# Attention results evacuated by ScalarE and normalised in place on GpSimd, thresholds on GpSimd, and both instruction orders written out as tables

## The chip, the cores and the metric

One core of a Trainium2 chip runs the whole program. The metric is device time in microseconds; lower is better. The five instruction queues that appear below are TensorE (PE), VectorE (DVE), ScalarE (ACT), GpSimd (POOL) and the DMA-issuing SyncE (SP).

## What is computed

```python
def _attn_ref(q, k, v, tau):            # q, k, v: 4 x 8 x 576 x 64
    scale = 1.0 / np.sqrt(q.shape[-1])
    scores = scale * np.matmul(q, k.transpose(0, 1, 3, 2))
    thresh = np.max(scores, axis=-1, keepdims=True) - tau
    scores = np.where(scores >= thresh, scores, -1000000000.0)
    scores = scores - np.max(scores, axis=-1, keepdims=True)
    attn = np.exp(scores)
    attn = attn / (np.sum(attn, axis=-1, keepdims=True) + 1e-09)
    return np.matmul(attn, v)
```

The result, as 2304 tokens of 512 numbers, goes through `g = max(h, 0) + alpha * min(h, 0)` with `h = x @ w_in`, then `g @ w_out`, and once more through such a pair of products (512 to 2048 to 512) with SiLU between them. All inputs are 32-bit floats.

## The kernel before

The program has two stages, one after the other. The first is attention, the second the four large matrix products ("the products stage").

**Attention.** Two heads of one batch entry make a pair; there are 16 pairs `i`, and each has nine tiles `t` of 64 query rows for both heads, so 144 units `u`. For one unit PE writes the scores into PSUM (`qkmm`, tile `s`; the tiles 0 to 7 go two at a time, tile 8 alone with twice the contraction), DVE scales them into SBUF and takes their extreme value (`maxi`, tile `x`), ACT takes the exponential (`expo`, tile `e`, or `z` for the ninth tile), and DVE compares `x` with the threshold and multiplies `e` by the result, with the row sum as a by-product (`mask`). The threshold itself is a sum of one or two columns, `thr`, on ACT. When a pair's nine masks are done, DVE takes reciprocals of the row sums in two pieces (`recip`), ACT copies them out into the tiles `rb` (`spread`, two pieces), PE transposes masked exponentials and reciprocals (`trans`), ACT copies the transposed blocks from PSUM (`copy`, tiles `pt` and `px`), PE multiplies by the values (`pv` in five steps, `pv8` for the ninth tile), and DVE multiplies the product in PSUM by the transposed reciprocals into the activations `X` (`evac`, and two 64x64 products `evac8`).

In the same stretch the weights of the first products are converted (`conv`: seven tiles, partly on POOL) and three sets of activations are split in a high and a low part (`piece`).

**The products stage** runs the 2304 tokens in three parts. Each product is made of three matrix multiplications of 384 columns over high and low parts; most 2x2 block products use seven block products in place of eight, with sums of blocks formed on DVE or POOL.

**What sets the order.** For attention PE's order is the string `ORDER` (`Q2:5` the scores of tiles 2 and 3 of pair 5, `T` a transposition, `P` a `pv` step); a list scheduler in the program, `plan`, places the other engines' work by due times, which the string `SHIFT1` corrects. For the products stage `plan_late` does the same with `SHIFT` and picks for each two-operand step marked BOTH whether DVE or POOL runs it (`SIDE` fixes some of them). Each engine then runs its instructions in that order, and semaphores hold what isn't ready.

Of the kernel before, what the change touches and what calls it, by code (L numbers as in the profile page):

```python
# [49 lines left out]
NRAW = 2  # L50
ST = ((False, True, True, True), (True,) * 4)
# [1322 lines left out]
```

## Time and profile before

| | us |
|---|---|
| median of 3 runs | 990.46 (988.98 to 991.07) |
| the profiled execution's own time | 991.97 |
| its span in the profile | 990.0 |
| busy: PE, DVE | 967.0, 857.6 |
| busy: ACT, POOL | 651.6, 295.8 |

The span starts with the first instruction of the program and ends with the last; the profiled execution lasts 2 us more. It stands 1.5 us above the median, so a difference that is worked out on the trace is taken off both alike. Attention takes the first 279 us, the products stage the rest. Busy time counts an instruction from its start to its end; neighbours on one engine overlap a little (two scalings of `x` start 0.74 us apart and last 0.82 us each), so a row's mean is somewhat more than what the next instruction waits for.

### The profile page before, as it was taken

The numbers are of one execution on the slowest core, as the hardware profiler recorded it, in microseconds if no ns is written. First come the engines' busy times: TensorE is split into PE (matmuls) and PEld (weight loads), VectorE is DVE, ScalarE is ACT, GpSimd is POOL, SyncE is SP. The second block draws the span as 40 slices with busy tenths as digits, with TensorE's granted clock in tenths as the row PEclk, the third lists the DMA queues.
The fourth block names the chain that finished last, engine by engine and source line by source line (L and its number), as shares of the span: only waits on it lengthen the run. The fifth ranks groups of instructions, "written<-read, shape, count | busy, mean of one in ns | idle before, by whom it ended". The sixth has DMA issues, their size and how long they took to land.

```text
span 990.0 us, 18130 instructions
## 1 busy us (share of the span) xinstructions
PE 967.0 (98%) x6781; PEld 857.7 (87%) x6781; DVE 857.6 (87%) x1740; ACT 651.6 (66%) x1179; POOL 295.8 (30%) x227
## 2 busy tenths in 40 slices
PE   8999899999999999999999999999999999999998
PEld 4555555555679999999999999999999999999998
DVE  6999999999879867988899999999788997788655
ACT  6997888989877666455555556777675555555442
POOL 0003111031033222344543344322333124544432
PEclk9999999999999999999999999999999999999999
DMA  3132322331365876677777887547766776655743
GB/s 117 47 113 75 127 68 93 109 91 47 117 250 228 287 265 215 237 249 263 260 240 237 260 267 273 180 183 274 277 238 220 262 261 254 230 213 196 249 160 112
DMA packets 46055, 194.11 MB, mean 196 GB/s; under 512 B 5392, under 2 KB 8592, under 8 KB 45968
## 3 DMA queue, kind: packets, MB, share of 16 engines
q1 hardware_dynamic: 43936, 187.97, 54.0%
q0 software_dynamic: 1728, 4.72, 2.5%
q8 instruction: 53, 0.87, 0.4%
q10 hardware_dynamic: 304, 0.28, 0.1%
q14 instruction: 34, 0.28, 0.1%
HBM read 150.48 MB, written 37.75 MB: 190 GB/s over the span
## 4 chain that ended last, share of the span: by engine, by line
PE 74%; DVE 14%; issue 5%; ACT 4%; DMA 3%; SPq 0%; DVEq 0%; ACTq 0%
PE ab L593 27%; PE c L593 17%; PE y L593 16%; PE y L1082 5%; DVE e L748 5%; DVE x L722 5%; PE s L708 4%; PE pv L815 3%; PE t L790 2%; DMA xs<-xd 2%; ACT e L735 1%; ACT pt L440 1%; DMA r<-r 1%; PE t L822 0%; DVE X L834 0%
## 5 line engine op out<-in xcount | busy, mean ns | idle before, releaser
L593 PE MATMUL ab<-xs,w 128*128 128x384 f32 x1728 | 316.0, 335 | 1.9 <-ACT su L440 1.3
L593 PEld LDWEIGHTS ab<-xs,w 128*128 128x128 f32 x1728 | 300.8, 188 | 3.7 <-ACT su L440 1.9
L593 PE MATMUL y<-g,w 128*128 128x384 f32 x840 | 158.8, 335 | 1.2 <-DVE X L1099 1.2
L440 ACT ACTIVATE g<-r 128x768 fp32r<-128x768 f32 (+1 forms) x143 | 112.9, 796 | 57.3 <-POOL r L1126 11.6
L593 PEld LDWEIGHTS y<-g,w 128*128 128x128 f32 x840 | 146.8, 188 | 1.5 <-DVE X L1099 1.5
L542 POOL TENSOR_TENSOR cw<-cw 128x128 f32<-128x128 f32 (+1 forms) x77 | 44.8, 581 | 253.6 <-DVE cw L528 158.5
L708 PE MATMUL s<-raw 64*128 64x288 f32 (+1 forms) x576 | 114.0, 432 | 5.0 <-DVE x L722 4.1
L722 DVE TENSOR_SCALAR_CACHE_REDUCE x<-s,nsc 128x576 f32<-128x576 f32 x144 | 112.9, 812 | 5.7 <-PE s L708 4.5
L593 PE MATMUL c<-g,w 128*128 128x384 f32 x612 | 115.7, 334 | 0.0
L748 DVE SCALAR_TENSOR_TENSOR e<-x,m,e 128x577 f32<-128x577 f32 x128 | 112.2, 907 | 2.9 <-ACT m L742 2.3
L440 ACT ACTIVATE su<-ab 128x384 f32<-128x384 f32 x144 | 69.4, 488 | 61.9 <-PE ab L593 55.7
L593 PEld LDWEIGHTS c<-g,w 128*128 128x128 f32 x612 | 107.0, 188 | 0.0
L735 ACT ACTIVATE e<-x,m 128x576 f32<-128x576 f32 x128 | 96.9, 777 | 15.2 <-DVE x L722 14.7
L1099 DVE TENSOR_TENSOR X<-y,X 128x384 f32<-128x384 f32 x150 | 81.7, 553 | 23.0 <-PE y L593 22.1
L1134 POOL TENSOR_TENSOR g<-r,g 128x768 fp32r<-128x768 f32 x41 | 75.9, 1863 | 82.7 <-ACT g L440 27.6
L708 PEld LDWEIGHTS s<-raw 64*128 64x128 f32 (+1 forms) x576 | 66.3, 191 | 36.1 <-DVE x L722 24.9
L545 POOL TENSOR_TENSOR w<-cw,w 128x896 fp32r<-128x896 f32 (+1 forms) x28 | 58.8, 2099 | 126.1 <-ACT w L440 110.2
L790 PEld LDWEIGHTS t<-ident,e 64*128 64x128 f32 x1152 | 51.3, 139 | 38.9 <-ACT pt L440 13.8
L1134 DVE TENSOR_TENSOR g<-r,g 128x768 fp32r<-128x768 f32 x80 | 78.2, 981 | 5.4 <-ACT g L440 5.3
L593 PE MATMUL c<-xs,w 128*128 128x384 f32 x432 | 81.9, 336 | 0.5 <-DMA xs<-xd 0.5
L593 PEld LDWEIGHTS c<-xs,w 128*128 128x128 f32 x432 | 75.4, 188 | 1.7 <-issue 0.8
L440 ACT ACTIVATE pt<-t 128x512 f32<-128x512 f32 x128 | 70.6, 591 | 7.8 <-PE t L790 7.8
(100 smaller groups left out, 1459.3 us busy)
## 6 DMA issues: line engine op xcount, KB each, us to landing
xs<-xd SPq DMA_DIRECT2D x126, 768.0 KB, 5.7
xd<-xs SPq DMA_DIRECT2D x42, 768.0 KB, 4.3
raw<-in_w1i SPq DMA_DIRECT2D x16, 512.0 KB, 5.2
raw<-in_w1o SPq DMA_DIRECT2D x16, 512.0 KB, 4.2
raw<-in_w2i SPq DMA_DIRECT2D x16, 512.0 KB, 4.9
raw<-in_w2o SPq DMA_DIRECT2D x16, 512.0 KB, 4.4
rv<-in_v SPq DMA_DIRECT2D x16, 480.0 KB, 4.2
raw<-in_q SPq DMA_DIRECT2D x15, 320.0 KB, 3.4
```

Of the source, the lines that this page charges most:

```text
L440: e.activation(out=dst, in_=src, func=AF.Copy)
L542: st.append((both_step if both else port_step)(256 if len(o.shape) == 3 else 128, ["cv", "ce", "ch"], ["ce"], lambda e=V, o=o, a=a, b=b, o ...
L545: st.append(both_step(512 if plain else 896, k + [(key, 0)], [(key, 0)], lambda e: e.tensor_tensor(out=z[:, 1], in0=x, in1=z[:, 0].bitcast ...
L593: T.matmul(bank, WT_[ws[c]][:, x, AI[a], :], xs[:, y, c, :], start=start and k == 0, stop=stop and k == 5, skip_group_check=True,)
L708: T.matmul(SP[u + k][:, hf, :S // 2], RAW[i][p, 0, q], RAW[i][p, 1, c], start=True, stop=True)
L722: V.tensor_scalar(out=x.rearrange("p (a b) -> p a b", a=2), in0=SP[u][:, :, :S // 2], scalar1=nsc, scalar2=None, op0=ALU.mult, op1=ALU.min ...
L735: A.activation(out=ES[u], in_=xts[u % XB][:, 1:S + 1], func=AF.Exp, bias=mcol(u, 0), scale=-1.0)
L748: V.scalar_tensor_tensor(out=e, in0=x, scalar=mcol(u, 1), in1=e, op0=ALU.is_le, op1=ALU.mult, accum_out=mcol(u, 2))
L790: T.transpose(TP[n][h][:, c * 64:c * 64 + 64], x[p], ident[p, p])
L1082: T.matmul(yt, wview(ws[f])[:, a, i * 128:(i + 1) * 128], half(gs[f, k])[:, c], start=n == 0, stop=n == 3 * G - 1)
L1099: V.tensor_tensor(out=dst, in0=src, in1=dst, op=ALU.add))))
L1134: add(*both_step(2 * HN, kr + kg, kg, lambda e: e.tensor_tensor(out=x[:, 1], in0=RP[n], in1=x[:, 0].bitcast(F32), op=ALU.subtract)))
```

## The change

- `evac` becomes a plain ACT copy from PSUM to `X`; the product with the reciprocals is made afterwards on POOL, in place in `X`, in pieces of up to 256 columns (`shares`, `norm`: 40 pieces over the 16 pairs). `evac8` becomes one ACT copy; its normalisation moves ahead of the transposition, where POOL multiplies the ninth tile's exponentials by its reciprocals (`norm8`, 16 times).
- `thr` moves from ACT to POOL (80 times). `recip` and `spread` are one instruction each per pair in place of two; the reciprocals' transposition is five blocks wide in place of six.
- POOL's other two-operand work in attention is cut in four: 28 parts of the seven weight tiles, 20 parts of the three activation splits (the sums of weight blocks stay whole).
- A two-operand POOL instruction in attention now waits for the last DVE instruction with two SBUF operands that the order puts ahead of it (`held`), as the products stage did already. 55 such waits are added, in front of 100 instructions.
- Before attention a few instructions run once on constant data (on `pr`), behind PE's nine idle matmuls; two exponentials on constant data at the start of ACT's queue go.
- `ORDER` is another string, and `plan` and `plan_late` no longer search: `replay` reads the order of all engines from `TABLE1` and `TABLE2`, and the side of each BOTH step from `SIDE`. In the products stage the instructions and their number are the same; 194 of the 528 BOTH steps stand on POOL against 183 before, PE's steps move by three places on average.

```diff
-SHIFT1 = (
+TABLE1 = (
+    "070308020t0x0u0-JpJq0y0+0zJr0B0v13141011Js160w0C1715At18JtJuJvAu191B1E12JwJx1A1FAw1G011C1J1DAx1NJyJz"
...
+    flat = [(*ops[n][:3], [rank[d] for d in ops[n][3] if d in rank]) for n in names]
+    ring = {rank["t", k]: [rank[x] for x in f] for k, f in enumerate(free)}
+    out, at = replay(flat, numbers(TABLE1), None, dict.fromkeys(("PE", "DVE", "ACT", "POOL", "SP"), 0.0), 0.0, names, ring)
...
-            A.activation(out=stat(i)[:, 1, a:z], in_=stat(i)[:, 0, a:z], func=AF.Identity, bias=ptau, scale=1.0)
+            P.tensor_scalar(out=stat(i)[:, 1, a:z], in0=stat(i)[:, 0, a:z], scalar1=ptau, scalar2=None, op0=ALU.add)
...
+        def recip(i):
+            V.reciprocal(stat(i)[:, 2], stat(i)[:, 2])
+
+        def spread(i):
+            RS[i] = rbp.tile([128, 8, 64], F32, tag="rb", name="rb")
+            A.activation(out=RS[i], in_=stat(i)[:, 2, 1:9].unsqueeze(2).to_broadcast([128, 8, 64]), func=AF.Copy)
+
+        def norm8(i):
+            e = EP[i, 4][:, 1:S + 1]
+            P.tensor_scalar(out=e, in0=e, scalar1=stat(i)[:, 2, 0:1], scalar2=None, op0=ALU.mult)
...
+        def evac(i):
+            for p, o, c, n in parts(i):
+                A.activation(out=X[p][:, pairs[i][1], o:o + n], in_=AV[i][:, c:c + n], func=AF.Copy)
...
+        def norm(i, p, o, c, n):
+            x = X[p][:, pairs[i][1], o:o + n]
+            return P.tensor_tensor(out=x, in0=x, in1=PT[i, "r"][:, :4].rearrange("p a b -> p (a b)")[:, c:c + n], op=ALU.mult)
...
+            A.activation(out=X[x][:, hp, c0:c0 + 64], in_=TP[bank[i, "r"]][1][:, 384:448], func=AF.Copy)
...
+        n = (512 if plain else 896) // parts
+        for c in (slice(i * n, (i + 1) * n) for i in range(parts)):
+            st.append(both_step(n, k + [(key, 0)], [(key, 0)], lambda e, c=c: e.tensor_tensor(
+                out=z[:, 1, c], in0=x[:, c], in1=z[:, 0, c].bitcast(F32), op=ALU.subtract)))
...
+        pq = [psS.tile([128, 2, 512], F32, tag="s", name="s") for _ in range(2)]
+        for hf in range(2):
+            for c in range(2):
+                for r in range(2):
+                    p = slice(r * 64, r * 64 + 64)
+                    T.matmul(pq[r][c * 64:c * 64 + 64, hf, :S // 2], pr[p, :64], pr[p, :S // 2], start=True, stop=True)
...
+        held = seen = None
+        for e, c, fn in todo:
+            x = fn()
+            if c == "DVE+":
+                held = x
+            elif c == "POOL+" and held is not seen:
+                tc.add_manual_dep(x.ins, held.ins.name, mybir.DependencyInfo(
+                    mybir.DependencyClass.Sync, mybir.DependencyReason.DATA), reason="port")
+                seen = held
```

The following rows are the instructions themselves in their order; line numbers are those of the kernel they belong to. On DVE, before, around the end of the third pair (L722 is `maxi`, L748 `mask`, L754 `recip`, L834 `evac`, L842 `evac8`):

```order
L722 TENSOR_SCALAR x_169,m<-s,nsc 128x576
L722 TENSOR_SCALAR x_172,m<-s,nsc 128x576
L842 TENSOR_TENSOR X_73<-t,px 64x64 x2
L748 SCALAR_TENSOR_TENSOR e,m<-x_169,m,e 128x577
L722 TENSOR_SCALAR x_175,m<-s,nsc 128x576
L748 SCALAR_TENSOR_TENSOR e,m<-x_172,m,e 128x577
L754 RECIPROCAL m<-m 128x8
L722 TENSOR_SCALAR x_169,m<-s,nsc 128x576
L722 TENSOR_SCALAR x_178,m<-s,nsc 128x576
L834 TENSOR_TENSOR X_73<-pv,px 128x512
L748 SCALAR_TENSOR_TENSOR z,m<-x_175,m,z 128x577
```

And on DVE with the change, at the same pair (L597 is `maxi`, L623 `mask`, L628 `recip`):

```order
L623 SCALAR_TENSOR_TENSOR e,m<-x_172,m,e 128x577
L623 SCALAR_TENSOR_TENSOR z,m<-x_175,m,z 128x577
L597 TENSOR_SCALAR x_175,m<-s,nsc 128x576
L628 RECIPROCAL m<-m 128x9
L597 TENSOR_SCALAR x_172,m<-s,nsc 128x576
L623 SCALAR_TENSOR_TENSOR e,m<-x_169,m,e 128x577
L623 SCALAR_TENSOR_TENSOR e,m<-x_178,m,e 128x577
L597 TENSOR_SCALAR x_169,m<-s,nsc 128x576
L597 TENSOR_SCALAR x_178,m<-s,nsc 128x576
```

`evac` and `evac8` have left DVE's queue, and what stands in it is scalings and masks, mostly two and two.

On POOL, before, the first two weight tiles (L542 are the sums of weight blocks, L545 the low part of a converted tile):

```order
L545 TENSOR_TENSOR w_76<-cw,w_76 128x896
L542 TENSOR_TENSOR cw<-cw 128x128
L542 TENSOR_TENSOR cw<-cw 128x256
L542 TENSOR_TENSOR cw<-cw 128x128
L545 TENSOR_TENSOR w_77<-cw,w_77 128x896
```

And on POOL with the change, at the second weight tile (L617 is `thr`, L636 `norm8`, L720 `norm`, L412 and L417 the former L542 and L545):

```order
L636 TENSOR_SCALAR z<-z,m 128x576
L412 TENSOR_TENSOR cw<-cw 128x128
L617 TENSOR_SCALAR m<-m,ptau 128x2
L412 TENSOR_TENSOR cw<-cw 128x256
L412 TENSOR_TENSOR cw<-cw 128x128
L617 TENSOR_SCALAR m<-m,ptau 128x2
L720 TENSOR_TENSOR X_73<-X_73,pr 128x256 x2
L617 TENSOR_SCALAR m<-m,ptau 128x2
L417 TENSOR_TENSOR w_77<-cw,w_77 128x224
L617 TENSOR_SCALAR m<-m,ptau 128x1
L417 TENSOR_TENSOR w_77<-cw,w_77 128x224 x2
```

POOL's queue was a few long products far apart; now thresholds, normalisations and parts of products share it, one behind the other.

## Rows read from the trace of the kernel before

**Rows 1.** Busy time by stretch: us, each engine's busy time, clock, DMA.

```profile
core 0: us, PE busy (x) PEld busy (x) DVE busy (x) ACT busy (x) POOL busy (x), PEclk, DMA share, GB/s
50.00:100.00 50.00, 47.77 (x495) 27.89 (x493) 49.43 (x126) 41.70 (x84) 9.53 (x8) 1.00 0.32 101
400.00:600.00 200.00, 200.00 (x1155) 199.98 (x1154) 181.04 (x337) 108.75 (x180) 82.04 (x66) 1.00 0.75 251
```

**Rows 2.** Groups of DVE by line, 0 to 300 us: busy, mean ns, idle before.

```profile
L722 DVE TENSOR_SCALAR_CACHE_REDUCE x<-s,nsc 128x576 f32<-128x576 f32 x144 | 112.9, 812 | 5.7 <-PE s L708 4.5 <-PE t L790 0.3
L748 DVE SCALAR_TENSOR_TENSOR e<-x,m,e 128x577 f32<-128x577 f32 x128 | 112.2, 907 | 2.9 <-ACT m L742 2.3 <-ACT e L735 0.2
L748 DVE SCALAR_TENSOR_TENSOR z<-x,m,z 128x577 f32<-128x577 f32 x16 | 12.9, 806 | 0.8 <-ACT m L742 0.8
...
L834 DVE TENSOR_TENSOR X<-pv,px 128x512 f32<-128x512 f32 (+4 forms) x24 | 11.4, 503 | 1.3 <-PE pv L815 1.3
...
L842 DVE TENSOR_TENSOR X<-t,px 64x64 f32<-64x64 f32 x32 | 7.0, 219 | 2.8 <-PE t L822 2.6
...
L754 DVE RECIPROCAL m<-m 128x8 f32<-128x8 f32 (+1 forms) x32 | 5.4, 176 | 0.2
```

**Rows 3.** Timeline: start, duration, engine, line; a long POOL product, then single scalings and masks.

```profile
7.42 0.82 DVE L722 TENSOR_SCALAR_CACHE_REDUCE x<-s,nsc 128x576 f32<-128x576 f32 x1 [2.65 <-PE s L708]
...
81.73 2.40 POOL L545 TENSOR_TENSOR w<-cw,w 128x896 fp32r<-128x896 f32 x1 [2.18 <-ACT w L440]
...
82.11 2.64 DVE L748 SCALAR_TENSOR_TENSOR e<-x,m,e 128x577 f32<-128x577 f32 x1
...
92.61 0.81 DVE L722 TENSOR_SCALAR_CACHE_REDUCE x<-s,nsc 128x576 f32<-128x576 f32 x1
...
93.35 0.81 DVE L748 SCALAR_TENSOR_TENSOR e<-x,m,e 128x577 f32<-128x577 f32 x1
...
269.36 0.82 DVE L748 SCALAR_TENSOR_TENSOR z<-x,m,z 128x577 f32<-128x577 f32 x1 [0.84 <-ACT m L742]
```

**Rows 4.** Groups of POOL by shape, 92.0 to 93.4 us.

```profile
L542 POOL TENSOR_TENSOR cw<-cw 128x256 f32<-128x256 f32 x1 | 0.7, 730 | 0.1
```

**Rows 5.** Groups of POOL by shape, 0 to 10 us: instructions with one operand.

```profile
masks.py:199 POOL TENSOR_SCALAR_AFFINE_SELECT ident<-ident 128x128 f32<-128x128 f32 x1 | 0.3, 291 | 0.1
...
L876 POOL TENSOR_SCALAR neg<-alp 128x16 f32<-128x16 f32 x1 | 0.2, 200 | 4.8 <-DMA alp<-in_alpha 4.8
```

**Rows 6.** Groups of ACT by line, 0 to 300 us.

```profile
L440 ACT ACTIVATE pt<-t 128x512 f32<-128x512 f32 x128 | 70.6, 591 | 7.8 <-PE t L790 7.8
...
L742 ACT ACTIVATE m<-m,ptau 128x2 f32<-128x2 f32 (+1 forms) x80 | 23.6, 294 | 5.3 <-DVE x L722 5.3
L760 ACT ACTIVATE rb<-m 128x512 f32<-128x512 f32 (+1 forms) x32 | 14.7, 468 | 5.9 <-DVE m L754 5.6
```

**Rows 7.** Timeline of PE: its first scores, then one step of each kind.

```profile
5.61 1.77 PE L708 MATMUL s<-raw 64*128 64x288 f32 x8 [0.40 <-DMA raw<-in_q]
...
261.86 1.19 PE L708 MATMUL s<-raw 64*128 64x288 f32 x8
...
262.88 0.66 PE L790 MATMUL t<-ident,e 64*128 64x64 f32 x16
...
263.48 1.08 PE L815 MATMUL pv<-pt,rv 128*64 128x512 f32 x4
...
264.49 1.24 PE L708 MATMUL s<-raw 128*128 128x288 f32 x4
...
265.66 0.72 PE L790 MATMUL t<-ident,e 64*128 64x64 f32 x16
...
278.75 1.33 PE L593 MATMUL c<-xs,w 128*128 128x384 f32 x6
```

**Rows 8.** PE's waits from 268 us on: engine, line, released by, us, times, longest.

```profile
PE ab L593 <- ACT su L440: 1.3, 2, 0.8
PE y L593 <- DVE X L1099: 1.2, 1, 1.2
```

More of the change, by code (lines that the diff above doesn't have):

```diff
@@ L50 @@
 NRAW = 2
+NS = 256
+N8 = 0.8
 ST = ((False, True, True, True), (True,) * 4)
@@ new lines, in numbers, with replay @@
+def numbers(text):
+    return [64 * CODE.index(a) + CODE.index(b) for a, b in zip(text[::2], text[1::2])]
+def replay(ops, order, side, lead, lag=0.0, names=None, ring=()):
+    at, port = dict(lead), {"DVE": 0.0, "POOL": 0.0}
+    home, end, out, last, before, tq = {"DVE+": "DVE", "POOL+": "POOL", "SWD": "POOL"}, {}, [], "", "", []
+    for i in order:
+        c, d, z, deps = ops[i][:4]
+        e = side[i] if c == "BOTH" else home.get(c, c)
+        tail = z - d
+        if c == "BOTH" and e == "POOL":
+            d, tail = d * POOL_RATE[0] + POOL_RATE[1], POOL_RATE[1]
+        deps = list(deps)
+        if i in ring:
+            deps += [ring[x][k] for k, x in enumerate(tq[:-3:-1])]
+            tq.append(i)
+        t = max([at[e]] + [end[j][e == end[j][2] == "PE"] for j in deps])
+        two = e in port and c != "SWD" and c != e
+        if two:
+            t = max(t, port["POOL" if e == "DVE" else "DVE"] + lag * (e == "POOL" and port["DVE"] > 0))
+        if e == "PE" and names:
+            n = names[i]
+            if mode(n) != last:
+                t = max(t, at[e] + SWITCH)
+                d += FIRST.get(n[0], 0.0)
+            elif n[0] == "qk" and before == "t":
+                d += 0.054
+            last, before = mode(n), n[0]
+        at[e] = t + d
+        if two:
+            port[e] = t + d
+        end[i] = (t + d + tail, t + d, e)
+        out.append((t, len(out), i, e))
+    return sorted(out, key=lambda x: x[:2]), at
@@ L235, with plan_late @@
+def plan_late(ops, lead):
+    return replay(ops, numbers(TABLE2), [{"p": "POOL"}.get(c, "DVE") for c in SIDE], lead, 0.1)
 class Track:
@@ L559, in xkeys, with piece @@
         return [("xs", slot, c) for c in range(2)]
-    def piece(p, name, slot, part=3, hi=False):
+    def piece(p, name, slot, part=3, hi=False, parts=1):
         def q(j, k):
@@ L570, in piece @@
         }.get(name, [])
+        n = max(1, parts // 2)
+        cuts = [(slice(None), slice(c, c + 1), slice(i * HN // n, (i + 1) * HN // n)) for c in range(2) for i in range(n)] if parts > 1 else [slice(None)]
         src = {"B11": b11, "B21": b21, "B22": b22, "T1": tB}.get(name, tA)
@@ L911, in attn_moe_moe @@
             op(("t", n), "PE", us, 1, need + [("t", n - 1)], lambda n=n: trans(n), us + 0.22)
-            free = {"e": [("pv", i - 2, KT - 1), ("pv8", i - 2)], "r": [("evac", i - 2), ("evac8", i - 2)]}.get(kind, [("pv", i - 2, KT - 1)])
+            free = {"e": [("pv", i - 2, KT - 1), ("pv8", i - 2)], "r": [("norm", i - 2, k) for k in range(4)] + [("pv8", i - 2)]}.get(kind, [("pv", i - 2, KT - 1)])
             for h in range(2):
@@ L921, in attn_moe_moe @@
                 op(("pv", i, kt), "PE", 0.857, 2, need, lambda i=i, kt=kt: pv(i, kt), 1.08)
-            op(("evac", i), "DVE", 0.62 if pairs[i][0] in (0, 3) else 0.74, -1, [("pv", i, KT - 1), ("copy", bank[i, "r"], 0), ("copy", bank[i, "r"], 1)], lambda i=i: evac(i), 0.78 if pairs[i][0] in (0, 3) else 0.9)
+            us = 0.48 if pairs[i][0] in (0, 3) else 0.57
+            op(("evac", i), "ACT", us, -1, [("pv", i, KT - 1)], lambda i=i: evac(i), us + 0.16)
+            for k, x in enumerate(shares(i)):
+                us = 0.17 + x[3] * 2.15e-3
+                op(("norm", i, k), "POOL+", us, -1, [("evac", i), ("copy", bank[i, "r"], 0), ("copy", bank[i, "r"], 1)], lambda i=i, x=x: norm(i, *x), us + 0.15)
         wdone = []
@@ L925, in attn_moe_moe, with normed @@
             after = [qk(WI + j * WS if j < WN else NU - WT)]
-            wdone.append(chain(("w", j), conv("wi" if j < 4 else "wo", 0, j % 4, 0), after))
-        src = [qk(NU - XO)] + [x for i in range(2 * HP) for x in (("evac", i), ("evac8", i))]
+            wdone.append(chain(("w", j), conv("wi" if j < 4 else "wo", 0, j % 4, 0, parts=4), after))
+        def normed(i):
+            return [("norm", i, k) for k in range(4)] + [("evac8", i)]
+        src = [qk(NU - XO)] + [x for i in range(2 * HP) for x in normed(i)]
         def keep(p, q, slot):
@@ L946, in attn_moe_moe @@
             steps.append(keep(p, q, slot))
-            chain(("xt", k), steps, src + [("late",)] + [x for i in range(2 * HP, 3 * HP) for x in (("evac", i), ("evac8", i)) if p])
+            chain(("xt", k), steps, src + [("late",)] + [x for i in range(2 * HP, 3 * HP) for x in normed(i) if p])
         for n in range(4):
```

502 lines of the change are left out of this document (163 added, 339 removed), and 28 rows, old and new, of the table ORDER.

## The prediction

> **What bounds the kernel now.** I read the stretches first. In the products stage PE is busy for all of the 200 us shown, at the full granted clock, while DVE, ACT and POOL have idle time; in attention the picture is another one: from 50 to 100 us DVE is busy 49.43 of 50 us, PE 47.77 and ACT 41.70, and POOL only 9.53 [rows 1]. So attention is DVE's stage. The groups of DVE say of what: 144 scalings and 144 masks, and beside them the evacuations and reciprocals; DVE's idle time in front of all of these is a few us [rows 2]. The first scaling starts at 7.42 us and the last mask ends at 270.2, a stretch of 262.8 us [rows 3]. PE then finishes the last pair, until 278.75 [rows 7], and from there on it hardly waits: its two largest waits behind 268 us are 1.3 and 1.2 us [rows 8]. The end therefore moves by what attention loses, as long as the products stage keeps its pace.
>
> One more thing is to be seen. A mask normally gives way to the next instruction after 0.74 us (93.35 less 92.61 is the same step for a scaling) and shows 0.81 or 0.82. At 82.11 a mask takes 2.64 us, and a POOL product of two operands that began at 81.73 ends at 84.13 [rows 3]. The mask, which reads two operands from SBUF, stood still until POOL was done. Over 128 masks the mean is 907 ns against 806 for the 16 of the ninth tiles [rows 2]; against the undisturbed 820 that is 128 x 0.087 = 11 us of DVE's stretch lost to POOL. Scalings, which read PSUM, show no such loss (mean 812).
>
> **What the change takes from DVE's stretch.** The 24 products of `evac` have 11.4 us, the 64 x 64 products 7.0, the 16 one-column reciprocals about half of 5.4 [rows 2]. One product of 0.7 us and two small ones of 0.5 us stand behind the last mask and are no part of it; 0.08 us of overlap comes off each of some forty of the others. 11.4 + 7.0 + 2.5 - 1.2 - 3 = 16.7, so 17 us go. The bounds are 15 (overlap everywhere) and 20 (none).
>
> The 11 us lost to POOL's long products go as well, and new losses come. POOL now has 28 parts of weight tiles, 20 of activation splits, 12 sums of weight blocks and 40 `norm` pieces, 100 instructions of two operands. One of 256 columns takes 0.73 us when left alone [rows 4]. In the order 55 groups of them wait for a mask or a conversion step, and the DVE instructions right behind that one are two scalings in most cases, 1.48 us, or one, 0.74. Groups of two pieces of 192 to 256 columns need 1.1 to 1.46 us in proportion to their width and fit with a start delay of 0.1 or miss by 0.1. If all fit, nothing is lost. If they fell anywhere, they would meet masks by these masks' share of the time, 144 x 0.74 of some 250 us or 43%: the 100 pieces are 192 columns wide on average, 0.55 us each in proportion, so 0.43 x 55 = 24 us. I take 4, close to the end where they fit, since the groups are cut to the length of the scalings.
>
> `thr`, 80 times on POOL, costs some 0.20 us like the 16-column instruction of one operand, against 0.294 on ACT [rows 5, 6]; `norm8` lies between 0.65 (the step from 16 to 128 columns, 0.09 us, extended to 576) and 1.4 us (the rate of the two-operand piece) [rows 4, 5]. Both lie beside DVE's work if a one-operand instruction does not hold a mask up; the trace of before has none beside a mask. I take 0; the other end is a rival below.
>
> **What it puts on the path.** At the start PE gets eight matmuls on constant data in front of the first scores. These scores took 1.77 us, where the same step later takes 1.19 [rows 7]; I take +0.7 us for the start, between 0 (they only move the slow first time forward into idle time) and 1.8. The two exponentials that ACT loses lie in the wait for the first scores: nothing.
>
> ACT gives up 23.6 us of thresholds and about a third of the 14.7 us of `rb` copies [rows 6]; it takes 24 copies of at most 0.59 us and 16 small ones of some 0.3, below 17 us in sum. It loses more than it gets, and was not the bound; nothing. The in-place products behind the last copy are wanted only when their part of the tokens is split, and the first part is complete long before: nothing, and 1.5 us (two pieces) if that cover were gone.
>
> PE is the engine that comes next. Steps of PE from start to start are 1.02 us for a pair of score tiles (262.88 less 261.86), 0.60 for a transposition, 1.01 for a `pv` step, 1.17 for a ninth tile [rows 7]. 64 x 1.02 + 16 x 1.17 + 80 x 0.60 + 80 x 1.01, and 0.6 for each of 16 transposed reciprocals and 16 `pv8`: 65 + 19 + 48 + 81 + 19 = 232 us. From 5.61 to 278.75, less four early products of 1.04 us, PE had 269 us for them, 86%. Take DVE's gain off and it has 247: 94%. PE, ACT and DVE also hold each other up (a scaling frees the bank that PE's scores need, a copy frees the transposition's bank), so waits of DVE, 9.4 us in sum in the rows of its masks and scalings before [rows 2], grow. I take +4, between 0 and 13 (the 269 us reduced to 256, if PE could not be filled over 91%).
>
> The products stage keeps its instructions, with another order. Its waits of 1.3 and 1.2 us [rows 8] could go, or others come. I take 0, between -4 and +5.
>
> **The sum**: -17 - 11 + 4 + 0 + 0.7 + 4 + 0 = -19.3 us. On the profiled execution's 991.97 that is 972.7; taken off the median of 990.46, 971.2. I forecast **971 us**, with its own range of 963 to 979.
>
> **The rivals.** *One-operand instructions of POOL hold masks up too.* For it: a mask did stand still beside POOL [rows 3]; against: every case seen had two operands on POOL. In the order, 54 of the 80 thresholds become ready when DVE has just begun a mask with another behind it. The threshold would run between the two, so the second starts 0.2 us late [rows 5]: 11 us. In 11 of the 54 the second mask needs just that threshold and waits for its release too, say 0.2 more: 2 us. Three of 16 `norm8` come ahead of two masks: 2 us. 971 + 15 = 986 us. The Trainium skill (SBUF — State Buffer, "SBUF: two separate sides") states that the shared pair of ports is locked for a whole instruction by a DVE instruction with two SBUF inputs against any GpSimd instruction that reads SBUF. By that page this rival holds, and its two-operand case agrees with the 2.64 us mask; no row shows the one-operand case.
>
> *PE takes over.* If PE cannot be filled more than the 86% of before, 232 / 0.86 = 270 us, no gain would be left; at 88%, 264 us against 269, 5 us are gained: 985 us. For it: the new order switches between kinds of PE work more often (245 times between scores, transpositions and `pv`, against 228). Against: PE's waits were mostly for DVE, whose load falls.
>
> *Better than the sum*: pieces fit entirely, the extra waits of 4 us stay away and the products stage loses its two waits: 971 - 4 - 4 - 3 = 960 us.
>
> *Slower: thresholds stuck in POOL's queue.* A piece holds POOL's queue until its mask is done, and 80 thresholds stand behind such pieces in the same queue; each is waited for by a mask on DVE, which again holds the next piece. It decides at 20 / 80 = 0.25 us per threshold. If each of the 55 groups delays one mask by 0.5 us (two thirds of a piece), 27 us are lost: 971 + 27 = 998 us. For it: before, a threshold on ACT cost DVE 2.3 and 0.8 us in sum, up to 1 us at a time [rows 2], and ACT didn't wait for masks. Against: the order puts most thresholds ahead of a piece or between two scalings.
>
> That the change does not do what it says is excluded: `evac` stands no longer in DVE's queue.
>
> **How the numbers follow.** Chances: forecast 0.57, one-operand lock 0.16, PE takes over 0.11, better 0.07, slower 0.09. The range, 960 to 988, holds the first three and part of the better case, and leaves out the slower one and the edges. Faster by over 0.2% (below 988.5, about what a measurement of this kernel can tell) is the first four less a little of the third: 0.88; slower (over 992.4) 0.09; between 0.03.
>
> **What would show it.** Right: the last mask ends near 251 us, masks of `e` have a mean of 0.83 to 0.86 us, POOL pieces of 256 columns 0.73 to 0.80, and PE's waits in the products stage sum to under 6 us. One-operand lock: thresholds on POOL have means well over 0.2 us, up to 0.7. PE takes over: DVE's idle time in front of scalings, released by PE's scores, is over 15 us. Slower: masks wait for POOL's `m`. Wrong altogether would be an unchanged end of attention, or waits in the products stage of over 10 us.

## The result, and the profile of the changed kernel

The changed kernel takes **978.96 us** (median of four runs, 978.03 to 979.5). The kernel before took 990.77 us beside it; the ratio is 0.9878, with a 95% interval of 0.9855 to 0.9901. The profiled execution is 978.03 us with a span of 975.9, against 991.97 and 990.0. It is faster by 1.2%, and 8 us slower than forecast. The medians lie 11.8 us apart and the two profiled executions 13.9, because the one of before stands 1.2 us above its median and the changed one 0.9 below; the traces below are of these executions.

The two stretches of [rows 1] read as follows in the changed kernel (start and end, length, busy time and instructions of each engine, granted clock, DMA share, GB/s):

```profile
50.00:100.00 50.00, 48.54 (x566) 29.24 (x564) 48.54 (x129) 45.66 (x85) 30.43 (x40) 1.00 0.35 120
400.00:600.00 200.00, 199.17 (x1145) 198.03 (x1144) 185.04 (x336) 109.16 (x184) 80.57 (x73) 1.00 0.73 245
```

From 50 to 100 us POOL went from 9.53 to 30.43 us of work, ACT from 41.70 to 45.66 and PE from 47.77 to 48.54, while DVE lost a little. All three of PE, DVE and ACT are now above 91%.

DVE's groups from 0 to 300 us, which answer [rows 2] (busy, mean ns, idle time before them and what ended it):

```profile
L597 DVE TENSOR_SCALAR_CACHE_REDUCE x<-s,nsc 128x576 f32<-128x576 f32 x144 | 112.4, 812 | 8.4 <-PE s L583 5.4 <-PE t L666 1.3
L623 DVE SCALAR_TENSOR_TENSOR e<-x,m,e 128x577 f32<-128x577 f32 x128 | 102.6, 829 | 8.4 <-POOL m L617 8.3
L623 DVE SCALAR_TENSOR_TENSOR z<-x,m,z 128x577 f32<-128x577 f32 x16 | 13.1, 816 | 0.5 <-POOL m L617 0.5
```

The evacuations are gone from this engine, and the masks' mean fell from 907 to 829 ns. But the idle time ahead of the masks rose from 2.9 to 8.4 us, and nearly all of it ends with a threshold on POOL. What POOL does in attention, in the same columns:

```profile
L617 POOL TENSOR_SCALAR m<-m,ptau 128x2 f32<-128x2 f32 x64 | 39.0, 611 | 55.5 <-DVE x L597 55.1
L636 POOL TENSOR_SCALAR z<-z,m 128x576 f32<-128x576 f32 x16 | 30.5, 1906 | 12.6 <-DVE m L628 8.6 <-ACT X L709 2.6 <-PE t L666 1.2
L720 POOL TENSOR_TENSOR X<-X,pr 128x256 f32<-128x256 f32 x16 | 12.3, 784 | 5.8 <-ACT X L709 3.5 <-DVE e L623 2.3
```

A threshold of two columns takes 611 ns in the mean, and one `norm8` 1906 ns. The products of 256 columns, at 784 ns, are near the 730 of [rows 4].

The waits that came with it, up to 262 us (engine, line, what released it, us in sum, times, longest):

```profile
DVE e L623 <- POOL m L617: 8.3, 19, 1.6
PE t L666 <- POOL z L636: 8.0, 10, 1.5
DVE x L597 <- PE s L583: 5.4, 9, 2.0
```

And from 255 us on, PE's largest waits, against the 1.3 and 1.2 us of [rows 8]:

```profile
PE t L666 <- ACT pr L310: 0.7, 1, 0.7
PE c L469 <- DVE X L999: 0.4, 1, 0.4
```

Set side by side, the two traces account for the whole difference in span, 14.1 us. The table adds up, over DVE's instructions from its first scaling to the end of its last mask, the time that each kind takes in the queue, and below it what lies outside that stretch.

| | before | after | difference, us |
|---|---|---|---|
| first scaling starts | 7.42 | 8.43 | +1.0 |
| `evac`, `evac8` and reciprocals on DVE | 19.6 | 2.3 | -17.3 |
| 144 masks, start to start | 120.0 | 111.8 | -8.2 |
| scalings and conversion steps | 115.8 | 117.4 | +1.6 |
| DVE's idle time (ahead of masks: 3.8, then 8.8) | 7.3 | 16.7 | +9.4 |
| last mask to PE's last attention product | 8.72 | 10.83 | +2.1 |
| from there to the last product | 707.6 | 704.9 | -2.7 |

The first five rows add up to 270.1 us and 256.6 us for the end of the last mask.

### The profile page after: what moved, and what is told of

Its sections match the earlier page's. It is cut to its first block, busy times and chain, and to the rows that moved or that the text cites. A ratio compares the mean times of both kernels' runs of the same rounds, so it can differ in the third digit from the quotient of the medians.

```text
span 975.9 us, 18268 instructions
## 1 busy us (share of the span) xinstructions
PE 958.3 (98%) x6763; PEld 852.7 (87%) x6765; DVE 836.7 (86%) x1660; ACT 629.2 (64%) x1120; POOL 382.2 (39%) x412
## 4 chain that ended last, share of the span: by engine, by line
PE 81%; DVE 7%; POOL 5%; issue 3%; ACT 3%; DMA 1%; DVEq 0%; POOLq 0%; ACTq 0%
PE ab L469 30%; PE c L469 18%; PE y L469 18%; PE y L983 5%; PE s L583 4%; PE pv L687 3%; DVE x L597 3%; POOL z L636 3%; DVE e L623 2%; PE t L666 2%; ACT e L610 1%; ACT pt L310 1%; POOL m L617 1%; POOL X L720 1%; DVE z L623 1%
## 5 line engine op out<-in xcount | busy, mean ns | idle before, releaser
L469 PE MATMUL ab<-xs,w 128*128 128x384 f32 x1728 | 327.3, 335 | 0.3 <-DMA xs<-xd 0.3
L469 PEld LDWEIGHTS ab<-xs,w 128*128 128x128 f32 x1728 | 301.9, 188 | 1.3 <-issue 0.6
L469 PE MATMUL y<-g,w 128*128 128x384 f32 x840 | 164.5, 335 | 0.1
L412 POOL TENSOR_TENSOR cw<-cw 128x128 f32<-128x128 f32 (+1 forms) x110 | 62.9, 572 | 226.8 <-DVE cw L398 72.4
L469 PEld LDWEIGHTS y<-g,w 128*128 128x128 f32 x840 | 147.2, 188 | 0.8 <-POOL g L1035 0.4
L310 ACT ACTIVATE g<-r 128x768 fp32r<-128x768 f32 (+1 forms) x143 | 111.8, 795 | 55.7 <-POOL r L1027 13.1
L597 DVE TENSOR_SCALAR_CACHE_REDUCE x<-s,nsc 128x576 f32<-128x576 f32 x144 | 112.4, 812 | 8.4 <-PE s L583 5.4
L469 PE MATMUL c<-g,w 128*128 128x384 f32 x612 | 119.4, 335 | 0.0
L1035 POOL TENSOR_TENSOR g<-r,g 128x768 fp32r<-128x768 f32 x45 | 83.1, 1848 | 89.9 <-ACT g L310 19.7
L623 DVE SCALAR_TENSOR_TENSOR e<-x,m,e 128x577 f32<-128x577 f32 x128 | 102.6, 829 | 8.4 <-POOL m L617 8.3
L469 PEld LDWEIGHTS c<-g,w 128*128 128x128 f32 x612 | 107.4, 188 | 0.1
L583 PE MATMUL s<-raw 64*128 64x288 f32 (+1 forms) x576 | 103.9, 422 | 2.0 <-DVE x L597 1.7
L310 ACT ACTIVATE w<-cw 128x896 fp32r<-128x896 f32 (+1 forms) x64 | 59.7, 933 | 44.7 <-POOL cw L412 28.7
L583 PEld LDWEIGHTS s<-raw 64*128 64x128 f32 (+1 forms) x576 | 61.1, 188 | 31.0 <-DVE x L597 20.3
L469 PE MATMUL c<-xs,w 128*128 128x384 f32 x432 | 85.2, 336 | 0.7 <-DVE X L999 0.4
L469 PEld LDWEIGHTS c<-xs,w 128*128 128x128 f32 x432 | 75.7, 188 | 1.2 <-DVE X L999 0.7
L1035 DVE TENSOR_TENSOR g<-r,g 128x768 fp32r<-128x768 f32 x76 | 73.5, 970 | 1.8 <-ACT g L310 1.7
```

The costliest lines, as they stand in the source:

```text
L310: e.activation(out=dst, in_=src, func=AF.Copy)
L412: st.append((both_step if both else port_step)(256 if len(o.shape) == 3 else 128, ["cv", "ce", "ch"], ["ce"], lambda e=V, o=o, a=a, b=b, o ...
L469: T.matmul(bank, WT_[ws[c]][:, x, AI[a], :], xs[:, y, c, :], start=start and k == 0, stop=stop and k == 5, skip_group_check=True,)
L583: T.matmul(SP[u + k][:, hf, :S // 2], RAW[i][p, 0, q], RAW[i][p, 1, c], start=True, stop=True)
L597: V.tensor_scalar(out=x.rearrange("p (a b) -> p a b", a=2), in0=SP[u][:, :, :S // 2], scalar1=nsc, scalar2=None, op0=ALU.mult, op1=ALU.min ...
L623: return V.scalar_tensor_tensor(out=e, in0=x, scalar=mcol(u, 1), in1=e, op0=ALU.is_le, op1=ALU.mult, accum_out=mcol(u, 2))
```

## The experiments

Each kernel below was run against the kernel before on the same chip, and the ratios are to that kernel, so they are to be compared with 0.9878. Prices in us are differences of medians to the 978.96 us of the changed kernel; worked out by the ratios they come out up to 2.4 us otherwise (17 for 18, 28 for 29, 18.5 for 16.2, 15 for 13). My theory at the start was that thresholds and `norm8` cost more on POOL than they would on ACT; the rival was that ACT has no room for them, and a third suspect was the order itself. Attention's new order was not run by itself, and no kernel put the evacuations back on DVE: what their leaving brought is read from the two traces, in the table above.

**Thresholds back on ACT.**

```diff
-P.tensor_scalar(out=stat(i)[:, 1, a:z], in0=stat(i)[:, 0, a:z], scalar1=ptau, scalar2=None, op0=ALU.add)
+A.activation(out=stat(i)[:, 1, a:z], in_=stat(i)[:, 0, a:z], func=AF.Identity, bias=ptau, scale=1.0)
```

> The changed kernel with the thresholds back on ScalarE, order tables kept. Theory (GpSimd thresholds wait beside a mask and masks then wait for them): DVE's 8.8 us of waits for POOL's m go, 3 us of waits for ACT's m come, attention ends some 4 us earlier, 975 us against 979. Rival (the three engines hold each other up, and any saving on one turns up as a wait for another): ScalarE has 15 us more in attention and 979 us stays within 2 us, with the waits moved to exponentials and copies.

996.94 us, ratio 1.0047 (1.0029 to 1.0064): 18 us slower than the changed kernel. DVE's waits up to 275 us:

```profile
DVE e L623 <- ACT m L617: 11.8, 14, 2.0
DVE e L623 <- ACT e L610: 8.4, 12, 1.1
```

Masks now wait 11.8 us for ACT's thresholds, more than for POOL's, and another 8.4 for exponentials. The thresholds' own group shows why ACT can't simply take 23.7 us of work more:

```profile
L617 ACT ACTIVATE m<-m,ptau 128x2 f32<-128x2 f32 (+1 forms) x80 | 23.7, 298 | 16.3 <-DVE x L597 16.0
```

In front of them ACT stands for 16.0 us waiting for DVE's scalings, with exponentials and copies queued behind. The order is the changed kernel's, written for thresholds on another engine, so this prices the placement within this order only.

**`norm8` on ACT, and both on ACT.**

```diff
-P.tensor_scalar(out=e, in0=e, scalar1=stat(i)[:, 2, 0:1], scalar2=None, op0=ALU.mult)
+A.activation(out=e, in_=e, func=AF.Copy, scale=stat(i)[:, 2, 0:1])
```

> The changed kernel with the normalisation of the ninth tile as a ScalarE activation with a per-row scale in place of the GpSimd instruction. Theory (one 1.73 us instruction on POOL is on the path of PE's transpositions and holds thresholds behind it): PE's 8.0 us of waits for POOL's z go, the step from the last mask to PE's last pv8 falls by 1 us, thresholds come earlier, total some 6 us less, 973 us. Rival (engines hold each other up): ScalarE gets 16 x 0.67 = 11 us more, PE's waits move to ScalarE's copies, 979 us within 2.

986.3 us, ratio 0.9942 (0.9921 to 0.9963), 7 us slower. An instruction of this kind takes 776 ns on ACT, much less than on POOL, and yet DVE's masks wait 9.7 us for exponentials:

```profile
L636 ACT ACTIVATE z<-z,m 128x576 f32<-128x576 f32 x16 | 12.4, 776 | 9.9 <-DVE m L628 9.9
DVE e L623 <- ACT e L610: 9.7, 10, 2.2
```

> Both moves at once: thresholds and ninth-tile normalisation on ScalarE, POOL has only two-operand pieces. Theory: gains add up to some 8 us, 971 us, unless ScalarE, with 26 us more, is full (its busy share in attention over 0.97). Rival: ScalarE is the bound and the kernel is slower than the changed one, 982 us or more.

1008.12 us, ratio 1.0161 (1.0138 to 1.0184), 29 us slower, a little more than the two apart (18 + 7). My theory fell: in this order each costs more on ACT than on POOL, and ACT was no slack engine. That moving work off it was part of the gain fits, but isn't shown apart from the order. Part of `norm8`'s price on ACT also came by PE's clock: from 182 to 185 and from 216 to 219 us the granted clock was 0.50 (1.2 of 2.4 GHz), each time behind a pause of PE of 1.6 us, and the changed kernel has no such fall in attention.

**The pieces don't wait for a mask.** The dependencies that put a two-operand POOL piece behind a mask are left out.

```diff
-            elif c == "POOL+" and held is not seen:
-                tc.add_manual_dep(x.ins, held.ins.name, ...)
-                seen = held
```

> The changed kernel without the waits of GpSimd's two-operand pieces for masks, order the same. Theory (the waits keep pieces beside scalings): masks of e, mean 829 ns now, rise to 870 to 900, 5 to 9 us on DVE, 985 us. Rival (the pieces' own inputs and their place in the queue do that already, or their waits cost as much as they save): mean under 845 ns and 979 us within 2, or less.

985.59 us, ratio 0.9934 (0.9914 to 0.9954), 6.6 us slower. The masks show where:

```profile
L623 DVE SCALAR_TENSOR_TENSOR e<-x,m,e 128x577 f32<-128x577 f32 x128 | 109.0, 878 | 8.2 <-POOL m L617 8.2
```

Their mean is 878 ns against 829, and the 144 masks take 119.0 us start to start against 111.8. These 7.2 us cover the whole loss (the span grew by 6.3); the waits for thresholds (8.2) are as in the changed kernel. The pieces' waits do what the prediction put on them.

**Without `norm8`.** The normalisation of the ninth tiles is left out.

```diff
-            P.tensor_scalar(out=e, in0=e, scalar1=stat(i)[:, 2, 0:1], scalar2=None, op0=ALU.mult)
```

> The changed kernel with GpSimd's norm8 left out and everything else in its place; the normalisation of the ninth tiles is not computed here. In the changed kernel norm8 takes 1.9 us each time, PE's transpositions wait 8.0 us for it in sum, and the last one lies between DVE's last mask and PE's end, which has grown from 8.7 to 10.8 us. Theory A (norm8's length is on the path, by PE's waits and by the thresholds queued behind it): the last mask comes 3 to 6 us earlier than 256.6 us and PE's end of attention another 2 us, so some 971 to 974 us against 979. Rival B (PE, ACT and DVE hold each other up anyway; the waits only change their name): the last mask stays within 2 us of 256.6, only the 2 us behind it go, 976.5 to 978.

964.55 us, ratio 0.9735 (0.9705 to 0.9764): 14.4 us faster, beyond both theories. The stretch shrank from 248.2 to 236.3 us, and the waits up to 250 us are:

```profile
PE s L583 <- DVE x L597: 1.7, 2, 0.9
PE pv L526 <- DVE cw L496: 1.2, 1, 1.2
...
DVE x L597 <- PE s L583: 4.7, 7, 2.7
...
DVE e L623 <- POOL m L617: 2.4, 12, 0.4
```

PE waits for nothing of weight any more, and the masks' wait for thresholds fell from 8.3 to 2.4 us although the thresholds stayed on POOL. So most of that wait was `norm8`, 1.9 us long, ahead of a threshold in POOL's queue. PE, from 50 to 200 us:

```profile
50.00:100.00 50.00, 49.74 (x580) 30.57 (x580) 48.62 (x133) 46.84 (x87) 25.84 (x39) 1.00 0.32 110
100.00:150.00 50.00, 49.83 (x541) 29.49 (x537) 49.61 (x135) 48.06 (x90) 27.08 (x46) 1.00 0.32 110
150.00:200.00 50.00, 49.96 (x583) 30.17 (x583) 48.90 (x131) 47.39 (x91) 20.22 (x38) 1.00 0.32 102
```

It is busy for 149.5 of 150 us. PE bounds attention once `norm8` is out of the way. Behind the last mask, though, less went than the 2 us that were expected: from there to PE's last attention product it took 9.9 us, against 10.83.

**No thresholds at all, by a mask on the exponential.** What is kept is the same set but for rounding: a scaled score is within tau of the row's minimum just when its exponential is at least exp(-tau).

```diff
+        A.activation(out=pe, in_=ptau, func=AF.Exp, scale=-1.0)
-            P.tensor_scalar(out=stat(i)[:, 1, a:z], in0=stat(i)[:, 0, a:z], scalar1=ptau, scalar2=None, op0=ALU.add)
-                out=e, in0=x, scalar=mcol(u, 1), in1=e, op0=ALU.is_le, op1=ALU.mult, accum_out=mcol(u, 2)
+                out=e, in0=e, scalar=pe, in1=e, op0=ALU.is_ge, op1=ALU.mult, accum_out=mcol(u, 2)
```

> The changed kernel with no thresholds at all: the mask compares the exponential with exp(-tau), one constant per partition, instead of the scaled score with minimum plus tau; same kept entries but for rounding. GpSimd loses its 80 additions; DVE's masks keep their form and length. In the changed kernel DVE's masks wait 8.8 us for thresholds (3.8 before the change for ACT's). Theory A (late thresholds on GpSimd are on the path): those 8.8 us go, less what PE and ACT then take back, so the stretch from the first scaling to the last mask shrinks from 248 to 240 to 243 us and the time is 970 to 974. Rival B (ACT or PE is the bound right behind, as the runs with work put back on ACT suggest): the masks then wait for the exponentials instead, and the time stays at 977 to 980.

970.38 us, ratio 0.9791 (0.9758 to 0.9825), 8.6 us faster, as theory A had it. Up to 255 us:

```profile
DVE e L623 <- ACT e L611: 1.1, 2, 0.7
...
PE t L666 <- POOL z L636: 5.8, 9, 1.0
```

The masks' wait for thresholds is gone and only 1.1 us for exponentials came in its place. PE still waits 5.8 us for `norm8`.

**Neither.** `norm8` and the threshold instruction are left out. This isn't the mask on the exponential: the mask compares `x` with the extreme value itself (`mcol(u, 0)` in place of `mcol(u, 1)`), so tau is not added.

> The changed kernel with neither thresholds nor norm8 on GpSimd: the normalisation of the ninth tiles and the addition of tau are not computed here, all else stays. Alone, the first left out gave 979 - 14.4 = 964.6 us, the other (by another comparison) 979 - 8.6 = 970.4. Theory A (the two delay different things and their prices add): 979 - 23 = 956 us, the stretch from the first scaling to the last mask near 229 us. Rival B (norm8 cost most of its 14 us by making thresholds late, so that the prices overlap, and PE, which is busy 99% of the time without norm8, is the bound behind both): 961 to 964 us, the stretch 233 to 236, DVE's masks waiting for nothing but DVE's scalings for PE's scores with over 6 us.

962.78 us, ratio 0.9691 (0.9666 to 0.9715). The prices don't add: once `norm8` is gone, leaving out the thresholds too brings 1.8 us on the medians (4.4 by the ratios), in intervals that overlap. The traces agree: the stretch from the first scaling to the last mask is 248.2 us in the changed kernel, 236.3 without `norm8`, 241.2 without thresholds and 233.8 with neither, so 14.4 us went where the two apart gave 11.9 and 7.0. Rival B was right, and masks wait for next to nothing:

```profile
L597 DVE TENSOR_SCALAR_CACHE_REDUCE x<-s,nsc 128x576 f32<-128x576 f32 x144 | 112.7, 814 | 9.0 <-PE s L583 6.3 <-PE t L664 1.4
L622 DVE SCALAR_TENSOR_TENSOR e<-x,m,e 128x577 f32<-128x577 f32 x128 | 100.2, 815 | 0.6 <-ACT e L610 0.2
```

What is left of DVE's idle time is mostly ahead of scalings, and 6.3 us of it is released by PE's scores.

**`norm8` on DVE**, with `V` in place of `P` in its line.

> The changed kernel with norm8 as the same instruction on DVE, in the place that GpSimd's had in the order. On GpSimd it takes 1.9 us and its removal was worth 14.4 us; on ScalarE the time was 986. On DVE a one-operand pass over 512 columns takes 0.46 to 0.52 us (the conversion steps) and a scaling of 576 columns 0.81, so 16 x 0.6 to 0.8, 10 to 13 us, are put into DVE's queue; it reads one operand from SBUF and can't be held up by GpSimd as a mask is. Theory A (the length of norm8 between the last mask of a pair and the transposition is what costs, and PE is the bound without it, so DVE has some idle time to take it): 964.6 + 7 to 10 = 972 to 975 us. Rival B (DVE's stage takes the whole 10 to 13 us, and scores wait for the scalings behind it): 975 to 979, no gain over GpSimd.

977.59 us, ratio 0.9858 (0.9829 to 0.9888), not to be told from the changed kernel. Rival B's time came, but not by its reason alone: the sixteen instructions took 9.9 us, yet one stretch stands out. In 1 us steps (same columns as the first fence), below the group itself:

```profile
L636 DVE TENSOR_SCALAR z<-z,m 128x576 f32<-128x576 f32 x16 | 9.9, 617 | 0.4
...
120.00:121.00 1.00, 0.03 (x1) 0.00 (x0) 1.00 (x4) 0.80 (x2) 0.15 (x1) 1.00 0.69 266
121.00:122.00 1.00, 0.00 (x0) 0.00 (x0) 1.00 (x3) 0.00 (x0) 0.92 (x2) 0.96 0.00 0
122.00:123.00 1.00, 0.52 (x8) 0.51 (x8) 1.00 (x2) 0.00 (x0) 0.11 (x1) 0.50 0.00 0
...
125.00:126.00 1.00, 1.00 (x6) 0.10 (x2) 0.32 (x2) 0.13 (x1) 0.53 (x2) 0.50 0.00 0
...
128.00:129.00 1.00, 1.00 (x8) 0.57 (x4) 0.00 (x0) 1.00 (x4) 0.00 (x0) 0.62 0.00 0
```

PE stood still for 2.45 us waiting for this `norm8`, which started at 121.36 us: the pair's reciprocals had started at 116.86, and three scalings, a mask and three conversion steps stood between in DVE's queue. PE's clock then fell to 0.50 (1.2 of 2.4 GHz) for about 7 us, and DVE in turn waited 3.9 us for late scores. By that wait the time might be some 4 us less (an estimate; it wasn't tried). The expectation was wrong that POOL can't hold this instruction up: eleven of the sixteen took 0.52 to 0.54 us, and five, all beside two-operand work of POOL, 0.70 to 1.07.

**Whole instead of pieces.** The low part of each weight tile in one POOL instruction at the place of the last of its four parts.

```diff
-            ... lambda e, c=c: e.tensor_tensor(out=z[:, 1, c], in0=x[:, c], in1=z[:, 0, c].bitcast(F32), op=ALU.subtract)
+            ... (lambda e: None) if c.stop < n * parts else lambda e: e.tensor_tensor(
+                out=z[:, 1], in0=x, in1=z[:, 0].bitcast(F32), op=ALU.subtract)
```

> The changed kernel with the low parts of the weight tiles done again by one whole GpSimd instruction each (seven of some 1.7 to 2 us) in place of the last of four parts, which waits for a mask as the part did; all else is the changed kernel's. Theory A (the pieces are what keeps GpSimd's two-operand work between two masks): each whole instruction runs over one scaling into a mask and holds it for 0.5 to 1.2 us, seven times, so masks of over 1.3 us come back and the time is 3 to 8 us over 979: 982 to 987. Rival B (DVE has idle time to take this, or the fewer starts and waits make up for it): 977 to 981 us.

985.9 us, ratio 0.9932 (0.9907 to 0.9957): 7 us slower, theory A's time by another way. The masks did not become longer (mean 829 ns again), because the next instruction in DVE's queue was a conversion step that wants the buffer which the long instruction reads:

```profile
142.59 2.09 POOL L417 TENSOR_TENSOR w<-cw,w 128x896 fp32r<-128x896 f32 x1
...
144.70 0.47 DVE L394 TENSOR_SCALAR cw<-raw 128x512 uint16<-128x512 uint16 x1 [2.60 <-POOL w L417]
```

DVE's waits for conversion steps rose from 1.3 to 6.0 us, and PE's for `norm8`, queued behind, from 8.0 to 11.5:

```profile
PE t L666 <- POOL z L636: 11.5, 9, 2.7
```

Behind the longest of these, 2.65 us up to 105.78 us, PE's granted clock stood at 0.50 from 107 to 110.5 us, so part of the price is the clock. So here the pieces are worth 5 to 7 us by work that is done earlier, three quarters of each tile; how much is the waits and how much the clock isn't told apart, and that the pieces also avoid a hold-up isn't shown by this run.

**The products stage's order alone**, in the kernel before (the table, the sides and the replay of the products stage, nothing of attention).

> The kernel before, with only the products stage taken in the changed kernel's order (its table of letters and its replay); attention is planned as before. On the traces the stretch from the last attention instruction of PE to its last product lasted 707.6 us before and 704.9 after the change. Theory A (the order of the products is worth these 2.7 us): 987.5 to 988.5 us against 991, with the two waits of 1.3 and 1.2 us gone. Rival B (the 2.7 us are a by-product of attention ending in another state, or of the runs): 990 to 992, and the two waits stay.

990.28 us, ratio 0.9992 (0.9974 to 1.001): by the runs, no difference that can be told. On the trace PE's last attention product to its last product is 705.5 us, against 707.6 before and 704.9 after, and PE's waits from 262 us on are

```profile
PE ab L594 <- DMA xs<-xd: 1.3, 1, 1.3
PE c L594 <- DVE X L1099: 0.2, 1, 0.2
```

The two waits of [rows 8] are gone and one for a DMA has come. The 2 us of the trace go with theory A, but the runs' interval holds both. The other traces speak for rival B: with this same order, and no fall of the clock, that stretch lasted 703.2 us (without `norm8`) to 706.9 (the last version below), so 2.7 us is less than it differs by without any change to it.

**Without the prelude on constant data.**

```diff
-        pr = rbp.tile([128, 592], F32, tag="pr", name="pr")
...
-                    T.matmul(pq[r][c * 64:c * 64 + 64, hf, :S // 2], pr[p, :64], pr[p, :S // 2], start=True, stop=True)
...
```

> The changed kernel without the eight matmuls and the three small instructions on constant data that it issues ahead of the first scores. The first scaling started at 7.42 us before and at 8.43 us after the change. Theory A (the prelude pushes the first scores back by about what I had put down for it): the first scaling starts at 7.4 to 7.7 us and the time is 0.7 to 1 us shorter, 978. Rival B (the first loads, or the slow first passage of the scores themselves, decide, and the prelude hides the latter): the first scaling stays at 8.2 us or later and the time is 979 to 980.

977.83 us, ratio 0.9871 (0.9844 to 0.9899). The first scaling started at 5.93 us instead of 8.43, but the stretch behind it grew from 248.2 to 249.3, and the runs can't tell the two kernels apart. The load of tau, which landed 0.9 us earlier in this execution, is no part of the 2.5 us: in both traces the first scaling is released by PE's scores, which start at 4.64 us here and at 7.08 behind the prelude. The last mask came 1.4 us earlier, and the products stage behind it took 706.5 us against 704.9. A single pair of executions says little about the start: with the prelude unchanged, the first scaling starts between 7.3 and 8.7 us in the traces of the other versions.

**A version that takes both off POOL and still computes everything.** On top of the mask on the exponential, the ninth tile is normalised behind its product, like the others: a sixth block in the transposed reciprocals, and two small products on POOL. The prelude is left out.

```diff
-            P.tensor_scalar(out=e, in0=e, scalar1=stat(i)[:, 2, 0:1], scalar2=None, op0=ALU.mult)
-                return out + [EP[i, 4][:, 513:641]]
+                return out + [EP[i, 4][:, 513:641], stat(i)[:, 2, 0:1].to_broadcast([128, 128])]
+            for h in range(2):
+                p = slice(h * 64, h * 64 + 64)
+                P.tensor_tensor(out=x[p], in0=x[p], in1=PT[i, "r"][p, 5, p], op=ALU.mult)
```

> A version that computes everything and takes both off GpSimd without giving them to another engine: masks compare the exponential with exp(-tau); the ninth tile is normalised behind its product instead of ahead of its transposition, by a sixth block in the transposed reciprocals and two GpSimd products of 64 x 64; the prelude on constant data is left out. Price on PE: 32 transpositions of 64 columns, 16 x 0.07 = 1.1 us; ACT copies 64 columns more, 16 x 2 x 0.05 = 1.6 us; GpSimd gets 32 products of about 0.3 us for 16 of 1.9. Theory A: as without norm8 and thresholds, plus these 1 to 3 us: 957 to 967 us. Rival B (the small products hold masks up, or ACT, which gets these columns, becomes the bound as when work was put back on it): 968 to 975 us, with masks of the main tiles at a mean over 850 ns.

965.86 us, ratio 0.9727 (0.9698 to 0.9756), **13 us faster than the changed kernel**, 3 us behind the kernel with neither, as theory A priced it. POOL's small products take 494 ns each, but nobody waits for them, and the masks' mean is 826 ns:

```profile
L728 POOL TENSOR_TENSOR X<-X,pr 64x64 f32<-64x64 f32 x32 | 15.8, 494 | 66.2 <-ACT X L725 64.9
L623 DVE SCALAR_TENSOR_TENSOR e<-e,pe 128x577 f32<-128x577 f32 x128 | 101.7, 826 | 0.8 <-ACT e L611 0.6
```

## Why the prediction was right in sign and 8 us short

**Evacuations, -17.** Measured: -17.3, on the traces. The step held, with the overlaps taken off as worked out.

**The hold-up of masks, -11 + 4 = -7.** Measured: -8.2. The run without the waits for a mask gives back 7.2 of them, so this was shown, not only argued. The e-masks' mean of 829 ns lies just under the 0.83 to 0.86 that I had named, and the 256-column pieces' 784 ns inside their 0.73 to 0.80.

**Thresholds and `norm8`, 0. This step failed.** Its words were that both lie beside DVE's work if a one-operand instruction doesn't hold a mask up. Masks wait by semaphore, though, and the thing waited for was late. `norm8` was estimated at 0.65 to 1.4 us and takes 1.73 when nothing of DVE's disturbs it, 1.9 in the mean; the upper bound was also worked out too low, since the 730 ns for 256 columns that it goes by make 1.64 us for 576 in proportion. It stands between a pair's last mask and its transposition on PE, which I had not said. On the last pair:

```profile
256.73 0.21 DVE L628 RECIPROCAL m<-m 128x9 f32<-128x9 f32 x1
...
256.74 2.38 PE L469 MATMUL ab<-xs,w 128*128 128x384 f32 x12
...
257.35 1.74 POOL L636 TENSOR_SCALAR z<-z,m 128x576 f32<-128x576 f32 x1
...
259.06 0.47 PE L666 MATMUL t<-ident,rb 64*128 64x64 f32 x8
```

This is only about 0.9 of the +2.1 behind the last mask. PE fills most of the time with products (`ab`, L469): from the last mask to its last attention product it is busy for 10.08 of 10.75 us, and in the six traces with `norm8` left out or moved off POOL the stretch of the table is still 9.9 to 10.0 us long. The rest goes with product steps that now fall behind the last mask: 18 of them, 6.3 us, against 13 and 4.5 before, of the same 24 that stand ahead of PE's last attention product. In all pairs together PE waited 8.0 us for `norm8`, and thresholds queued behind it reached their masks late. Leaving it out is worth 14.4 us, leaving out the thresholds 8.6, both 16.2.

**The rival of the one-operand lock** was half right. Thresholds did come to a mean of 0.61 us, the sign I had named for it. The timeline shows the direction:

```profile
12.80 0.82 DVE L623 SCALAR_TENSOR_TENSOR e<-x,m,e 128x577 f32<-128x577 f32 x1
...
12.98 0.79 POOL L617 TENSOR_SCALAR m<-m,ptau 128x2 f32<-128x2 f32 x1 [2.59 <-DVE x L597]
...
13.81 0.82 DVE L623 SCALAR_TENSOR_TENSOR e<-x,m,e 128x577 f32<-128x577 f32 x1 [0.18 <-POOL m L617]
...
43.49 0.29 POOL L617 TENSOR_SCALAR m<-m,ptau 128x2 f32<-128x2 f32 x1
```

Beside a scaling a threshold takes 0.29 us (26 of the 80 are near that). When it starts just behind a mask's start it takes 0.79, to about 0.15 us past that mask's end (42 of the 80). The mask itself keeps its 0.82. So the mask held up the threshold, and the next mask lost 0.18 here only because it needed just that threshold. The Trainium skill (SBUF — State Buffer, "SBUF: two separate sides") states that the shared pair of ports is locked for a whole instruction by a DVE instruction with two SBUF inputs against any GpSimd instruction that reads SBUF. The threshold's 0.79 agrees with it. What I had made of it, that the threshold would then delay the second mask by its own length, did not show for thresholds: of the 38 masks that stood right behind a mask beside which a threshold had started, 26 began without any gap, and the other 12 waited for a threshold. It showed on three masks for the long `norm8`, by 0.1 to 0.5 us, for instance here:

```profile
40.71 2.11 POOL L636 TENSOR_SCALAR z<-z,m 128x576 f32<-128x576 f32 x1 [2.57 <-ACT X L709]
41.14 1.29 DVE L623 SCALAR_TENSOR_TENSOR e<-x,m,e 128x577 f32<-128x577 f32 x1
```

Each of the three masks ended about 0.38 us before `norm8` did on the trace, so it was not kept out for the whole of that instruction.

**Waits, +4.** Measured: +9.4, of which 5.0 ahead of masks (thresholds, the step above), 3.4 ahead of scalings, most of it by PE's scores, and 1.1 ahead of conversion steps. Without the first, the +4 would have held. "PE takes over" did not happen in the changed kernel, where the wait for scores is 5.4 us and not 15. In the versions where nothing stands in its place (without `norm8`, with neither, and the last one) it is what happens next: PE is busy for 149.5 of the 150 us from 50 to 200, though the wait for scores stays at 4.7 to 7.8 us there, far from the sign that I had named.

**ACT, nothing.** The sum was right that ACT loses more than it gets. "It was not the bound" was too easy: the runs that gave it back 24 and 12 us of work lost 18 and 7, in an order that was not made for it.

**Start, +0.7**: measured +1.0, within the 1.4 us by which the start differs between traces. **Products, 0**: -2.7 on the traces, within my bounds and within what that stage differs by from trace to trace with one and the same order. **"Slower"**, thresholds stuck in POOL's queue, had the right mechanism at 5 us instead of 27: behind `norm8` more than behind pieces.

So -17.3, -8.2, +1.0, +9.4, +2.1, -2.7 and 1.6 for scalings and conversion steps give the -14.1 us, 5.2 less than the -19.3. `norm8` and the thresholds cost 5.9 of it (5.0 ahead of masks, 0.9 behind the last one); product steps behind the last mask and longer scalings and conversion steps cost 2.8, for which the sum had no term. The products stage's 2.7 us paid for part of that, which is luck: no step foresaw it, and the run of its order can't show it. The rest of the 8 us, some 2.5, is the profiled executions' distance from their medians. The time of 978.96 us lies at the very edge of the forecast's own range of 963 to 979.

## What to carry to other kernels

Work moved to an idle engine isn't free when somebody waits for its result: ask for each instruction who is next to want it, and how long it takes on that engine, before putting it at nothing. Here, doing without an instruction (a threshold folded into a constant comparison, a normalisation moved behind the product) was worth more than any placement of it that was tried: on ACT, DVE and POOL `norm8` gave 986, 978 and 979 us, folded away with the thresholds 966. When three engines are above 90% in a stage, removing a wait gains only until the next of them is full, so prices of single edits don't add.

## What the runs showed of the hardware

- A GpSimd instruction with a scalar per row, 128x576 from SBUF to SBUF in f32, took 1.73 us undisturbed, 3.0 ns a column; the two-operand piece of 256 columns 0.73 to 0.78 us, some 2.9 to 3.1 ns. The first of these took 0.62 us in the mean on DVE (0.52 to 0.54 in eleven of sixteen cases), and 0.78 on ACT.
- A one-operand GpSimd instruction of two columns took 0.29 us beside a DVE scaling and 0.79 beside a mask.
- PE's granted clock fell to 0.50 for some 3 to 7 us within attention in five traces, mostly behind pauses of PE: of 2.65 us (whole instead of pieces), 2.45 us (`norm8` on DVE, where a wait of 3.9 us on DVE followed), 1.6 us (`norm8` on ACT, twice), and 1.2 us in the kernel before. Not every such pause was followed by a fall: the changed kernel has pauses of 1.26, 1.44 and 1.45 us in attention and no fall there. The kernel before, in the columns of the first fence:

```profile
123.00:124.00 1.00, 1.00 (x10) 0.71 (x7) 1.00 (x4) 1.00 (x3) 0.00 (x0) 0.50 0.15 61
```
